# Mixer turn split in two portions per step, its first transposes in TensorE's given order

## The chip, the cores and the metric

The kernel runs on one core of one Trainium2 chip. The metric is the device time of one execution in microseconds (us). Engines are named as in the profile: PE is TensorE (matrix multiplications and transposes), PEld its weight loads, DVE is VectorE, ACT is ScalarE, POOL is GpSimd, SP issues DMA transfers.

## The reference, cut to what matters

Eight batches, eight heads of 64, 576 positions. Attention keeps, for each query, the scores that are at least its 32nd largest; what comes out (x, 576 by 512 for a batch) goes through a phase mixer.

```
scores = q @ k.T / 8;  kth = 32nd largest of each row
attn = exp(scores - max) where scores >= kth, else 0;  attn /= sum + 1e-9
x = (attn @ v), heads side by side                    # 576 x 512 per batch
theta = x @ w_theta
zr, zi = x * cos(theta), x * sin(theta)
y = w_tok_r @ zr + w_tok_i @ zi                       # over the 576 positions
u = x + y
out = u + max(u @ w_ch, 0)
```

## The kernel before

**Attention.** The work runs in units. A unit is one block `j` of 128 queries of a pair of heads `p` (five blocks, the last with 64 queries), so a batch has 20 units. `pipeline()` makes one step per unit; in step `i` the unit `i+3` gets its scores (`scores`, L259, copied out of PSUM by ACT in L268) and is folded on VectorE (`fold`, L295 to L298), unit `i+1` has its candidates picked (L303), unit `i` has its threshold found (`threshold`, L319 and L325), unit `i-1` is masked and exponentiated (L349, L351, L361), and unit `i-2` is turned: `turn` transposes the weights of each head on TensorE (`pt`, L376, four transposes, and the copy `at` out of PSUM by ACT, L378; `pq`, L386, for the rest) and calls `between()` after each of its two parts. `mix_values` multiplies by the values (`px`, L406).

**The mixer.** When a batch's 20 units are through, `mixer(...)`, a generator, is put into the list `running`. `between()` calls `advance(RATE / 2)`, so the mixer of the batch before advances twice in a step. Each call adds 4.25 to a budget, and the generator is resumed as long as the budget is above zero; each `yield` gives back the price of what has just been issued. A call to `between()` with what is issued in it is called a portion here.

The mixer has two stages. The first, called the turn here (the loop over `k`), runs over five blocks of 128 positions (the last has 64):
- the turn there: `px_s`, L595, four transposes that bring a block of x from channels to positions, into a PSUM buffer; then `normalize`, L494, on VectorE, which divides by the sums and frees that buffer;
- the turn back: `turn_back`, four transposes `px_t`, L509, and the copy `xt` by ACT, L510, which frees that buffer;
- the angles: `angles`, `pth`, L532 (L536 for the last block), four matmuls in float32 on the block that was turned back; `fraction` (L548 on ACT, L549 on VectorE) takes out whole turns.

When all five blocks are through, `trig` takes sines and cosines (L556 to L564). The second stage is the two products, 72 matmuls `py` (L647) and 32 matmuls `po` (L674) of one unit of price each, every one counted twice in the trace.

In each `k` the order before is: turn there of block `k`, turn back of block `k-1`, fraction of `k-3`, angles of `k-2`, and one `yield` of 2 or 9. Counted out with the budget, the portions of a mixer before are: 1: there 0, 1, 2, back 0, 1, angles 0; 4: there 3, back 2, angles 1; 6: there 4, back 3, angles 2; 8: back 4, angles 3; 10: angles 4; 12: the last fraction, trig, and the first four `py`. The other portions issue nothing of the mixer.

**What sets the order.** The framework's planner sorts each engine's instructions at compile time, by priority (the program's order; a mixer's instructions stand 100 places earlier, `M_REST`) and by its own times of when an instruction could start. Each engine then runs its list in that order. Instructions that got the same mark keep the program's order among themselves: `fixed` marks on TensorE the `pt` transposes, and through `fill` the angles, `py` and `po` of all mixers but the last. The transposes `px_s` and `px_t` carry no mark: the planner places them. ACT's exponentials and sines have a mark of their own (`tabled`).

**Buffers.** `pt`, `pq`, `px_s` and `px_t` share one PSUM pool, `ps_t`, of two buffers. `px`, `pth`, `py` and `po` share `ps_m`, two buffers. The scores have `ps_s`, two buffers.

**The last batch's mixer** has nothing beside it. It works with split operands (`split`), three matmuls for each one of the others, its turn back makes the parts `x_hi` (ACT, L513) and `x_lo` (VectorE, L516), and none of its instructions is marked.

Of the kernel before, what the change touches and what calls it, by code (L numbers as in the profile page):

```python
# [18 lines left out]
P = 128  # L19
# [3 lines left out]
AHEAD = 3  # L23
S_LATE = 0
RATE = 8.5
ORDER = "PTUFKSTVMXZ"
FOLDS = 4
BESTS = 4
# [16 lines left out]
def topk_attention_phase_mixer(  # L45
# [11 lines left out]
    nc = tc.nc  # L57
# [5 lines left out]
    NJ = S // P  # L63
# [22 lines left out]
    ident = const.tile([P, P], F32, name="ident")  # L86
# [86 lines left out]
    def later(n):  # L173
        return tc.high_priority(offset=-n)
# [253 lines left out]
    def two_blocks(tag, n, width, name, bufs=2):  # L428
        blocks = []
        while len(blocks) < n:  # L430
            t = wk2.tile([P, 2, S], F32R, tag=tag, name=name, bufs=bufs)
            blocks += [t[:, 0, :width], t[:, 1, :width]]
        return blocks[:n]
# [5 lines left out]
    def halve_weights(key):  # L439
        n, width = len(wts[key]), wts[key][0].shape[-1]  # L440
        hi = two_blocks("e", n, width, "w_hi", EBUFS)
        lo = []
        for c in range(n):
            if key == "th" and c == 0:
                lo.append(wk2.tile([P, S], F32R, tag="pen", name="w_lo", bufs=1)[:, :width])
            else:
                lo.append(weight_tile(F32R, width))
            halve(hi[c], lo[c], wts[key][c], nc.scalar.copy, nc.vector.tensor_sub if key == "ch" else nc.gpsimd.tensor_sub)
        w_parts[key] = hi, lo
# [3 lines left out]
    def mixer(bt, split=False, beside=False):  # L453
        bq, xt, sums, sums_rem = bt["bq"], bt["xt"], bt["sums"], bt["sums_rem"]
# [16 lines left out]
        fill = fixed if beside else lambda ins: None  # L471
# [16 lines left out]
        def normalize(k, px):  # L488
            rows, parts = (P, 1) if k < NJ else (REM, folds)
            for a in range(parts):  # L490
                cols = slice(a * DM // parts, (a + 1) * DM // parts)
                out = xs[k][a * D : a * D + rows, : DM // parts]
                hs = slice(cols.start // D, cols.stop // D)
                nc.vector.tensor_tensor(  # L494
                    out.rearrange("p (h d) -> p h d", d=D),
                    px[:rows, cols].rearrange("p (h d) -> p h d", d=D),
                    rinv[:rows, k, hs].unsqueeze(2).to_broadcast([rows, hs.stop - hs.start, D]),
                    op=ALU.mult,
                )

        def turn_back(j):
            rows, parts = (P, 1) if j < NJ else (REM, folds)
            m = NB // parts
            for a in range(parts):
                sl = slice(a * D, a * D + rows)
                pt = ps_t.tile([P, NB, P], F32, tag="t", name="px_t")
                with later(M_PE):
                    for p in range(m):
                        nc.tensor.transpose(pt[:, p, :rows], xs[j][sl, p * P : p * P + P], ident[sl, sl])  # L509
                nc.scalar.copy(xt[:, a * m : a * m + m, j * P : j * P + rows], pt[:, :m, :rows])  # L510
                if split:
                    cs = slice(j * P, j * P + rows)
                    nc.scalar.copy(x_hi[:, a * m : a * m + m, cs], pt[:, :m, :rows])  # L513
                    for p in range(a * m, a * m + m, 2):
                        pp = slice(p, p + 2)
                        nc.vector.tensor_sub(x_lo[p // 2][:, :, cs], xt[:, pp, cs], x_hi[:, pp, cs].bitcast(F32))  # L516

        def angles(j):
            th[j] = ps_m.tile([P, 512], F32, tag="m", name="pth")
            cs = slice(j * P, j * P + P) if j < NJ else slice(NJ * P, S)  # L520
            mm = []
            for p in range(NB):
                if split:
                    x = u_hi[p][:, cs], u_lo[p][:, cs]
                    mm += passes(*x, *(w[p] for w in w_parts["th"]))
                else:
                    mm.append((xt[:, p, cs], wts["th"][p]))
            with later(M_PE):
                for i, (l, r) in enumerate(mm):
                    pos = dict(start=(i == 0), stop=(i == len(mm) - 1), skip_group_check=True)  # L530
                    if j < NJ or split:
                        fill(nc.tensor.matmul(th[j][: l.shape[-1]], l, r, **pos))  # L532
                    else:
                        for a in range(2):
                            fill(
                                nc.tensor.matmul(  # L536
                                    th[j][a * D : a * D + D, :HD], l, r[:, a * HD : a * HD + HD], **pos
                                )
                            )

        def fraction(j):
            whole = wk2.tile([P, S], F32, tag="ot", name="whole", bufs=1)[:, :DM]
            if j == NJ:
                last[0] = whole
            _, zr, _ = spots(j)
            n = zr.shape[-1]
            m = zr.shape[0]
            nc.scalar.activation(whole[:m, :n], th[j][:m, :n], AF.Identity, bias=magic[:m])  # L548
            nc.vector.scalar_tensor_tensor(  # L549
                zr, whole[:m, :n], MAGIC, th[j][:m, :n], op0=ALU.subtract, op1=ALU.subtract  # L550
            )

        def trig(js):
            for j in js:
                x, zr, zi = spots(j)
                tabled(nc.scalar.activation(zi, zr, AF.Sin, scale=-TWO_PI))  # L556
                nc.scalar.activation(zr, zr, AF.Abs)
                tabled(nc.scalar.activation(zr, zr, AF.Sin, scale=-TWO_PI, bias=half_pi[: zr.shape[0]]))
                nc.gpsimd.tensor_mul(zr, x, zr)
                if split and j == NJ:  # L560
                    nc.vector.tensor_mul(z[REM : 2 * REM, 2 * NJ], x, zi)
                    halve_z(2 * NJ)
                    continue
                nc.gpsimd.tensor_mul(x if j < NJ else zi, x, zi)  # L564
                if split:
                    halve_z(NJ + j)
                    halve_z(j)
                if j == NJ:
                    for i in range(2):
                        for a in range(2):  # L570
                            nc.sync.dma_start(
                                z[i * D : i * D + D, 2 * NJ, a * HD : a * HD + HD], spots(j)[1 + i][a * D : a * D + D]
                            )
# [6 lines left out]
        if split:  # L580
            halve_weights("tok")
            halve_weights("ch")
            for i, n in enumerate(QN):
                t = wk2.tile([P, 2, NJ, n], F32R, tag=f"at{i}", name="z_hi", bufs=1)
                flat = t.rearrange("p a b n -> p (a b n)").rearrange("p (k d) -> p k d", d=DM)
                z_hi.extend(flat[:, k] for k in range(flat.shape[1]))
            z_lo += two_blocks("kh", NJ, DM, "z_lo") + two_blocks("q2", NJ, DM, "z_lo")
            z_lo.append(wk2.tile([P, S], F32R, tag="lo1", name="z_lo")[:, :DM])
        for k in range(NJ + 4):
            if k <= NJ:  # L590
                rows = P if k < NJ else REM
                px = ps_t.tile([P, DM], F32, tag="t", name="px_s")
                with later(M_PE):
                    for p in range(NB):
                        nc.tensor.transpose(px[:rows, p * P : p * P + P], xt[:, p, k * P : k * P + rows], ident)  # L595
                normalize(k, px)
            if 0 <= k - 1 <= NJ:
                turn_back(k - 1)
            if 0 <= k - 3 <= NJ:
                fraction(k - 3)  # L600
            if 0 <= k - 2 <= NJ:
                angles(k - 2)
            yield (2 if k <= NJ + 1 else 0) + (7 if 0 <= k - 2 <= NJ else 0)
        trig(range(NJ + 1))
        yield 0

# [83 lines left out]
    def pipeline():  # L690
# [46 lines left out]
        for i in range(total + 3):  # L737
# [4 lines left out]
            def keep():  # L742
                u = unit(i - 3)
                if u:
                    keep_values(u)
                    if u.j == NJ and u.p == NPAIR - 1:
                        done = B - 1 - u.bq
                        running.append(mixer(u.batch, done == 0, done > 0))

            def ahead():  # L750
# [9 lines left out]
                "Z": lambda: list(parts),  # L760
                "U": lambda: last and turn(last, unit(i - 3), lambda: advance(RATE / 2)),
                "K": keep,
# [4 lines left out]
            }  # L767
            for c in ORDER:
                steps[c]()
# [90 lines left out]
```

## Time and profile before

| what | us |
|---|---|
| median of 3 runs (1256.29 to 1263.52) | 1259.68 |
| the profiled execution, its own time | 1256.43 |
| its span, first to last instruction | 1254.7 |
| TensorE matmul busy | 1138.1 |
| VectorE busy | 1117.9 |
| ScalarE busy | 1016.3 |
| GpSimd busy | 686.5 |

Busy times are those of the whole span; the first 180 us also hold the preparation of weights and the first batch, the last 70 us the mixer of the last batch. Seven mixers run beside the attention of the next batch. A wait is idle time of an engine ahead of an instruction, with the one that released it.

### The profile page before, as it was taken

To read this page: it belongs to the slowest core of one execution; us is meant where nothing else is said; L and a number is where in the kernel's file an instruction comes from. 1 tells how busy PE (TensorE), PEld (TensorE's weight loads), DVE (VectorE), ACT (ScalarE), POOL (GpSimd) and SP (SyncE) were. 2 spreads that over 40 slices of the span, in tenths; PEclk is the share of its full clock that TensorE was granted. 3 is DMA by queue.
4 is the path that set the end of the run, shared out by engine and by line. 5 is a ranking of instruction groups with operands and counts; after the bars stand their busy time and mean duration, and the time that the engine had idled before them with its cause. 6 is when DMAs were issued, how large, how long until landed. Compare 5 with 4: busy or idle time off the path is not lost.

```text
span 1254.7 us, 22863 instructions
## 1 busy us (share of the span) xinstructions
PE 1138.1 (91%) x6293; PEld 847.9 (68%) x6293; DVE 1117.9 (89%) x5018; ACT 1016.3 (81%) x2098; POOL 686.5 (55%) x958
## 2 busy tenths in 40 slices
PE   4676678999899997999989999999989998899998
PEld 3454455777557775677757776677757775577688
DVE  7999999999998999889998989988999989995363
ACT  5799998897689977898779968898789977898361
POOL 2678875665456634566445644656455644557340
PEclk9767789999899999999999999999999999999999
DMA  6544542333323233333323333332323333210101
GB/s 165 128 131 135 152 109 53 94 86 101 89 67 76 62 109 96 78 83 86 91 52 94 86 104 87 85 90 59 102 72 95 86 94 97 68 27 11 39 1 41
DMA packets 71017, 106.12 MB, mean 85 GB/s; under 512 B 13920, under 2 KB 32608, under 8 KB 70880
## 3 DMA queue, kind: packets, MB, share of 16 engines
q1 hardware_dynamic: 70880, 104.57, 31.6%
q8 instruction: 52, 0.85, 0.3%
q14 instruction: 85, 0.70, 0.2%
HBM read 38.40 MB, written 9.44 MB: 38 GB/s over the span
## 4 chain that ended last, share of the span: by engine, by line
PE 41%; DVE 28%; ACT 18%; DMA 4%; POOL 4%; issue 3%; SPq 1%; ACTq 0%; DVEq 0%; POOLq 0%
PE py L647 13%; PE pth L532 7%; DVE best L319 6%; DVE lst L325 6%; PE px L406 5%; PE ps_score L259 5%; DVE lst L303 5%; ACT e L361 5%; PE pt L376 4%; ACT pen L349 3%; DVE lo L296 3%; ACT e L268 3%; PE po L674 2%; POOL e L351 2%; DVE ps_score L295 2%
## 5 line engine op out<-in xcount | busy, mean ns | idle before, releaser
L351 POOL TENSOR_TENSOR e<-e,pen 128x576 f32<-128x576 f32 x288 | 365.8, 1285 | 129.8 <-ACT pen L349 127.2
L319 DVE MAX8 best<-lst 128x8 f32<-128x102 f32 (+3 forms) x1152 | 287.2, 291 | 9.7 <-POOL lim L330 9.2
L647 PE MATMUL py<-w,z 128*128 128x288 f32 x1008 | 265.5, 407 | 0.6 <-ACT xt L418 0.6
L361 ACT ACTIVATE e<-e,lim 128x576 f32<-128x576 f32 x288 | 225.0, 783 | 26.4 <-POOL e L351 24.4
L349 ACT ACTIVATE pen<-e,lim 128x576 bf16<-128x576 f32 x288 | 210.5, 775 | 31.8 <-POOL lim L330 31.4
L325 DVE MATCH_REPLACE8 lst<-best,lst 128x102 f32<-128x102 f32 (+2 forms) x864 | 232.4, 277 | 0.1
L259 PE MATMUL ps_score<-kh,q 128*128 128x288 f32 x512 | 185.5, 377 | 31.8 <-ACT e L268 14.6
L303 DVE MAX8 lst<-lo 128x8 f32<-128x72 f32 (+1 forms) x864 | 210.1, 295 | 0.0
L647 PEld LDWEIGHTS py<-w,z 128*128 128x128 f32 x1008 | 182.2, 190 | 41.2 <-ACT xt L418 1.3
L376 PE MATMUL pt<-ident,e 128*128 128x128 f32 x1152 | 181.1, 283 | 27.0 <-ACT e L361 14.8
L376 PEld LDWEIGHTS pt<-ident,e 128*128 128x128 f32 x1152 | 140.5, 145 | 66.3 <-ACT e L361 18.1
L268 ACT COPY e<-ps_score 128x576 f32<-128x576 f32 x256 | 160.7, 640 | 29.6 <-PE ps_score L259 24.0
L378 ACT COPY at<-pt 128x512 f32<-128x512 f32 x256 | 148.2, 589 | 36.1 <-PE pt L376 35.5
L406 PE MATMUL px<-at,vt 128*64 128x320 f32 (+1 forms) x1024 | 164.0, 437 | 5.6 <-ACT at L381 3.1
L259 PE MATMUL ps_score<-kl,q 128*128 128x288 f32 x512 | 152.5, 312 | 0.4 <-DMA kl<-raw 0.4
L259 PEld LDWEIGHTS ps_score<-kh,q 128*128 128x128 f32 x512 | 101.6, 198 | 61.8 <-ACT e L268 22.3
L406 PEld LDWEIGHTS px<-at,vt 128*64 128x64 f32 x1024 | 79.4, 145 | 68.7 <-issue 15.1
L674 PE MATMUL po<-xt,w 128*128 128x288 f32 x448 | 124.0, 408 | 1.0 <-DVE ot L628 0.8
L296 DVE TENSOR_TENSOR lo<-ps_score,e 128x576 f32<-128x576 f32 (+1 forms) x160 | 110.2, 689 | 0.0
L532 PE MATMUL pth<-w,xt 128*128 128x512 f32 x224 | 109.7, 623 | 0.0
L259 PEld LDWEIGHTS ps_score<-kl,q 128*128 128x128 f32 x512 | 102.7, 201 | 8.6 <-issue 3.7
L295 DVE TENSOR_TENSOR ps_score<-ps_score,e 128x288 f32<-128x288 f32 (+1 forms) x160 | 68.3, 427 | 37.8 <-ACT e L268 35.3
(130 smaller groups left out, 1914.4 us busy)
## 6 DMA issues: line engine op xcount, KB each, us to landing
kh<-hi SPq DMA_DIRECT2D x124, 144.0 KB, 2.8
kl<-raw SPq DMA_DIRECT2D x124, 144.0 KB, 2.7
raw<-in_qT_dram SPq DMA_DIRECT2D x31, 288.0 KB, 2.9
raw<-in_kT_dram SPq DMA_DIRECT2D x31, 288.0 KB, 3.2
q<-hi SPq DMA_DIRECT2D x62, 144.0 KB, 2.7
q<-raw SPq DMA_DIRECT2D x62, 144.0 KB, 2.7
vt<-in_v_dram SPq DMA_DIRECT2D x32, 256.0 KB, 3.6
out_dram<-ot SPq DMA_DIRECT2D x28, 288.0 KB, 2.1
```

What stands on the lines that cost most here:

```text
L259: nc.tensor.matmul(out[:, at : at + n], l, r, start=(i == 0), stop=(i == len(mm) - 1), skip_group_check=True)
L268: nc.scalar.copy(u.x[:, :, keys], u.ps[:, :, :HS])
L303: nc.vector.max(u.lst[:, w, QS + i * 8 : QS + i * 8 + 8], u.lo1[:, w, lo:hi])
L319: nc.vector.max(top[:, w, best], part[w])
L325: nc.vector.match_replace(out=rest, in_to_replace=top[:, w, best], in_values=part[w], imm_value=LOWEST)
L349: nc.scalar.activation(pen[:, w], u.x[:, w], AF.Relu, bias=u.lim[:, w, 0:1], scale=-STEEP)
L351: nc.gpsimd.tensor_sub(u.x[:, w], u.x[:, w], pen[:, w])
L361: nc.scalar.activation(u.x[:, w], u.x[:, w], AF.Exp, bias=u.lim[:, w, 1:2], scale=SCALE, accum_out=acc)
L376: fixed(nc.tensor.transpose(pt[:, c], e[:, w, at0 : at0 + P], ident))
L406: nc.tensor.matmul(px[sl, :n], pr["vt"][:, kb, sl], pr["at"][:, a, kb], start=(kb == 0), stop=False, skip_group_check=True)
L532: fill(nc.tensor.matmul(th[j][: l.shape[-1]], l, r, **pos))
L647: fill(nc.tensor.matmul(py[:, :HS], l, r, start=(i == 0), stop=(i == len(mm) - 1)))
```

## The change

The turn's loop is issued in two portions per step. The first has the turn there of block `k`, the fraction of block `k-3` and the angles of block `k-2`; the second has the turn back of block `k-1`. Each gives back `TURN`, 4.25, all that a call adds. The transposes of the turn there get the mark `fixed`, through `fill`, in all mixers but the last.

Counted out in the same way, the portions become: 1: there 0; 2: there 1, back 0; 3: there 2, angles 0; 4: back 1; 5: there 3, angles 1; 6: back 2; 7: there 4, angles 2; 8: back 3; 9: angles 3; 10: back 4; 11: angles 4; 12: the last fraction, trig, and the first five `py`. In the last mixer only the order in which the loop issues its work is another.

```diff
@@ -23,6 +23,7 @@
 AHEAD = 3
 S_LATE = 0
 RATE = 8.5
+TURN = 4.25
 ORDER = "PTUFKSTVMXZ"
@@ -586,21 +587,23 @@
         for k in range(NJ + 4):
             if k <= NJ:
                 rows = P if k < NJ else REM
                 px = ps_t.tile([P, DM], F32, tag="t", name="px_s")
                 with later(M_PE):
                     for p in range(NB):
-                        nc.tensor.transpose(px[:rows, p * P : p * P + P], xt[:, p, k * P : k * P + rows], ident)
+                        fill(nc.tensor.transpose(px[:rows, p * P : p * P + P], xt[:, p, k * P : k * P + rows], ident))
                 normalize(k, px)
-            if 0 <= k - 1 <= NJ:
-                turn_back(k - 1)
             if 0 <= k - 3 <= NJ:
                 fraction(k - 3)
             if 0 <= k - 2 <= NJ:
                 angles(k - 2)
-            yield (2 if k <= NJ + 1 else 0) + (7 if 0 <= k - 2 <= NJ else 0)
+                yield TURN
+            if 0 <= k - 1 <= NJ:
+                turn_back(k - 1)
+            yield TURN if k <= NJ + 1 else 0
         trig(range(NJ + 1))
         yield 0
```

## Rows read from the trace of the kernel before

**Rows 1.** The page's first part: busy us, share of the span, instructions.
```profile
span 1254.7 us, 22863 instructions
...
PE 1138.1 (91%) x6293; PEld 847.9 (68%) x6293; DVE 1117.9 (89%) x5018; ACT 1016.3 (81%) x2098; POOL 686.5 (55%) x958
```

**Rows 2.** Windows: the turns of the mixers beside attention; busy us, PEclk granted share.
```profile
178.40:231.90 53.50, 45.58 (x232) 29.21 (x232) 51.90 (x230) 47.96 (x95) 34.65 (x45) 0.94 0.29 75
331.70:380.50 48.80, 43.63 (x227) 27.31 (x226) 46.12 (x208) 38.52 (x77) 27.26 (x38) 0.93 0.33 79
478.90:525.80 46.90, 41.58 (x222) 26.26 (x221) 42.73 (x189) 35.12 (x70) 23.61 (x31) 0.96 0.32 79
625.70:672.50 46.80, 42.22 (x228) 27.77 (x228) 44.90 (x204) 36.72 (x73) 25.22 (x35) 0.96 0.35 87
769.70:814.60 44.90, 42.01 (x226) 26.95 (x225) 44.66 (x202) 36.13 (x73) 24.55 (x33) 0.96 0.36 89
910.90:955.90 45.00, 41.15 (x231) 26.73 (x230) 44.37 (x195) 38.76 (x77) 26.76 (x35) 1.00 0.35 88
...
sum 332.50, PE 297.33 PEld 190.92 DVE 320.35 ACT 269.72 POOL 186.71; mean PE 42.48 PEld 27.27 DVE 45.76 ACT 38.53 POOL 26.67
```

**Rows 3.** Windows between those turns (231.9 to 1054.6, six stretches), summed.
```profile
sum 590.30, PE 577.40 PEld 452.46 DVE 548.87 ACT 501.47 POOL 319.60; mean PE 96.23 PEld 75.41 DVE 91.48 ACT 83.58 POOL 53.27
```

**Rows 4.** TensorE's waits, whole span: us in total, times, longest us.
```profile
PE px_s L595 <- DVE z L494: 6.7, 6, 3.1
PE px_s L595 <- ACT at L378: 4.6, 7, 2.0
...
PE pt L376 <- ACT xt L510: 3.8, 6, 1.3
PE px_t L509 <- DVE z L494: 3.4, 3, 1.7
PE pt L376 <- DVE z L494: 3.4, 3, 2.8
PE px_t L509 <- ACT xt L510: 3.2, 2, 2.3
...
PE pq L386 <- DVE end L494: 2.5, 2, 2.3
...
PE px_s L595 <- ACT xt L510: 2.0, 2, 1.3
PE pq L386 <- ACT xt L510: 2.0, 2, 1.3
```

**Rows 5.** Timeline of TensorE in the second mixer's turn: start, us.
```profile
335.87 0.66 PE L509 MATMUL px_t<-ident,z 128*128 128x128 f32 x4 [1.45 <-DVE z L494]
337.49 0.84 PE L595 MATMUL px_s<-ident,xt 128*128 128x128 f32 x4 [0.97 <-DVE z L494]
339.28 0.47 PE L509 MATMUL px_t<-ident,z 128*128 128x128 f32 x1 [0.94 <-ACT xt L510]
339.54 1.91 PE L532 MATMUL pth<-w,xt 128*128 128x512 f32 x2
...
352.20 3.60 PE L532 MATMUL pth<-w,xt 128*128 128x512 f32 x8
```

**Rows 6.** VectorE's waits, whole span: us in total, times, longest us.
```profile
DVE ps_score L295 <- ACT e L268: 35.3, 30, 3.7
...
DVE z L494 <- PE px_s L595: 5.9, 6, 2.4
```

**Rows 7.** Windows: the last mixer's turn; columns as in rows 2.
```profile
1187.00:1204.70 17.70, 16.93 (x91) 13.20 (x91) 10.67 (x20) 12.95 (x23) 2.60 (x2) 1.00 0.01 1
```

**Rows 8.** Timeline of the last mixer's turn, around one turn back.
```profile
1194.79 0.58 ACT L510 COPY xt<-px_t 128x512 f32<-128x512 f32 x1
...
1195.25 0.60 ACT L513 CAST x_hi<-px_t 128x512 fp32r<-128x512 f32 x1
...
1196.15 0.74 DVE L516 TENSOR_TENSOR x_lo<-xt,x_hi 128x256 fp32r<-128x256 f32 x2
```

## Prediction

> **What bounds the kernel now.** I began with the page: TensorE and VectorE are busy 91% and 89% of the span [rows 1], so neither is plainly the bound, and the stages have to be taken apart. I cut the span into windows: the seven turns that run beside attention, and what lies between them. Between the turns TensorE is busy 577.40 of 590.30 us and VectorE 548.87 [rows 3]: there TensorE sets the pace, with 13 us idle in six stretches, and VectorE waits for scores (the copy L268 behind TensorE's products, 35.3 us over the span) [rows 6]. In the turns it is the other way round on paper: TensorE is busy 297.33 of 332.50 us, so it is idle for 35.2 us, and VectorE is busy 320.35, idle for 12.15 [rows 2]. A turn stage is thus one in which both are nearly full, VectorE a little more.
>
> What TensorE waits for in the turns is read from its waits. The nine rows in which the turn's own work is late, or makes others late, add up to 31.6 us [rows 4]; the last mixer can hold no more than 0.77 of it, all its idle time [rows 7], so these waits are nearly all of the 35.2 us idle in the seven turns. They fall into three kinds:
> - The chain without distance, 21.2 us: the turn there waits for a buffer that `normalize` frees (6.7) or that a turn back's copy frees (2.0), the turn back for `normalize` (3.4) or for a copy (3.2), and `pt` and `pq` stand behind a late `normalize` (3.4 and 2.5).
> - `pt` and `pq` waiting for the copy L510 to free a buffer, 3.8 and 2.0, 5.8 together.
> - The turn there waiting for the copy of `pt`, 4.6 in 7 waits.
>
> The timeline shows why the first kind arises: portion 1 issues three turns there, two turns back and the first angles at once, and each stands behind the one before: 1.45, 0.97 and 0.94 us idle within 4 us [rows 5].
>
> A second loss hangs on it. In the same place two angle matmuls take 1.91 us, while eight take 3.60 us some 12 us later, 0.95 against 0.45 each [rows 5]: TensorE runs at the lower of its two levels, 1.2 instead of 2.4 GHz. The granted clock is 0.94, 0.93, 0.96, 0.96 and 0.96 in the first five turns, 1.00 in the sixth [rows 2]. Missing share times length gives 3.2, 3.4, 1.9, 1.9 and 1.8, 12.2 us of full-speed work lost. In the second turn it fell right after the gaps of portion 1.
>
> **The change part by part.** No instruction is added or removed on any engine. Trig, with its work on GpSimd and its DMA issues on SP, stays in portion 12, so neither queue is passed; ten turns (five there, five back) and their angles are issued in other portions.
>
> 1. *The chain gets distance.* Angles 0 came in the portion of their own turn back; now each block's angles stand one portion behind its turn back, and its turn back one to three portions behind its turn there. A turn lasts 47.5 us on average for 12 portions [rows 2], so a portion is about 4 us of cover, against waits of 0.9 to 3.1 us [rows 4, 5]. Blocks 1 to 4 had more portions between turn back and angles before than after (two or three, now one), so not all of this is won. Of the 21.2 I take two thirds, -14. The ends are 0 (the cover isn't there) and -21.2.
> 2. *`pt` and `pq` behind the turn back's copy.* The turn back still sits next to `pt` or `pq` and uses the same two buffers. I leave it: 0. Ends -5.8 and +5.8 (as often again, since a turn back now has a portion to itself in front of `pq`).
> 3. *The turn there in given order.* It can no longer be placed early; it comes right behind a `pt` and needs the other of the two buffers, which the copy of an earlier `pt` must have freed. Behind it stand, in TensorE's order, the angles and the next `pt`, and behind that ACT's copy and `px`. Seven waits took 4.6 us, 0.66 each [rows 4]; there are 35 such turns. I take twice as many as now: +4.6. Ends: none left, -4.6, and all 35 at 0.66, 23 in all, +18.4.
> 4. *The clock.* If gaps of portion 1 go, the lower level should go with most of them. The sixth turn has 3.85 us idle at 1.00 [rows 2], so gaps need not bring it down. I take half, -6; ends 0 and -12.2. The Trainium skill (TensorE: Matmul & The Clock Gate, Part 1) says that a monitor sets the array's rate by how busy it has been lately; that fits these rows, and by it all 12.2 us would come back once the array stays busy, which would make the forecast some 6 us lower. The sum does without it.
> 5. *The end of the turn.* Angles 4 move from portion 10 to 11, while trig and the first `py` stay in 12. Between angles 4 and the next unit's `pt`, one `pt` less and one `py` more are issued. I take 0; it lies within the uncertainty of item 3.
> 6. *The last mixer.* Angles now go ahead of the turn back of the next block, so for every second block TensorE may stand through that block's copy, `x_hi` and `x_lo`: from 1194.79 to 1196.89, 2.1 us [rows 8]. Two blocks can meet it, +4.2; the planner can place an idle transpose there, and TensorE is idle for 0.77 us in that turn now [rows 7], the most that could be won. I take +1.5; ends -0.8 and +4.2.
>
> TensorE in the turns: -14 + 0 + 4.6 - 6 = -15.4 us. Not all of it reaches the end: VectorE has only 12.15 us free in these windows [rows 2], and I cut the gain there: -12. With the last mixer -10.5. Against the profiled execution's own time, 1256.43 (its span and 1.7 us around it), that is 1245.9. This execution lies 3.25 below the median of the runs, 1259.68; on the median the forecast is 1249.
>
> **The rivals.**
>
> *VectorE is the bound in the turn, and nothing comes through.* It is busy 96% of these windows, and in the fifth 44.66 of 44.90 us [rows 2]; TensorE's time won there would be spent waiting for a folded unit to free the scores' buffers. Against it: between the turns VectorE has 41.4 us free [rows 3], and a TensorE that leaves the turn earlier starts the products earlier. Then only the turns in which VectorE has room give anything: the second and third, 2.7 and 4.2 us idle. The time would be 1253 to 1260, say 1257. The Trainium skill (Trainium Kernel Development and Optimization, Performance Expectations) says that a matmul's busy time is a poor measure and the weight loads' busy share a good one. By that TensorE is loaded to 57% in the turns (190.92 of 332.50) and to 77% between them, and it wouldn't be the bound in the turn. Chance 0.17.
>
> *The split doesn't happen on the engine.* `px_t` carries no mark, and the planner may put it right behind `px_s` again. The waits then change places. Two or three us less, 1257 as well. Chance 0.09.
>
> *The given order costs more than the distance gives: slower.* The place is the turn there behind `pt`. Gains of items 1 and 4 are 20 us; divided by 35 that is 0.57 us. From an average added wait of 0.57 us at each turn there it decides, and the waits seen are 0.66 on average and 2.0 at the longest [rows 4]. `normalize` stands in VectorE's order, and where the transposes come late VectorE waits too (5.9 us in 6 waits now) [rows 6], in a stage in which it has nothing to spare. At 0.9 us each, 31.5 - 20 and the last mixer's 1.5 give +13, 1273; at 0.7, 1266. For it speaks that a marked instruction can't be moved around a late one; against it that the angles behind the turn there give `normalize` 3.6 us of cover [rows 5] before the next `pt` asks for a buffer. Chance 0.20.
>
> **How the numbers follow.** The forecast has 0.54. A measurement of this kernel can tell some 0.5% from no change, 6.3 us: faster is below 1253.4, slower above 1266.0. The first two rivals mostly fall in between, the third mostly above. So faster 0.54, same 0.26, slower 0.20. The forecast's own range is 1238 (all of items 1 and 4 less item 3's 4.6 is 28.8; 12.15 of it in the windows, half of the rest by VectorE's room between the turns, and 0.8 in the last mixer: 21.3) to 1255 (half of item 1, no clock: -10.6 + 4.6 + 1.5). For 8 in 10 I leave out the best tenth below 1239 and the worst above 1268, which takes in the first two rivals and the near part of the third.
>
> **What would show it.** Right: the rows of `px_s`, `px_t`, `pt` and `pq` waiting for L494 and L510 fall from 27 to about 13 us; the granted clock in the first five turns is 0.98 or more; windows of a turn get 1 to 3 us shorter, and VectorE's waits for L268 between the turns don't grow. Item 3 is wrong if `px_s` waits for L378 more than 10 us. The first rival is right if TensorE's waits for the fold (L298) grow in the turns by what the others lose. Item 6 is wrong if the last 68 us of the span move by more than 4. The prediction as a whole is wrong if TensorE's idle time in the turns stays above 30 us, or if it falls and the span doesn't.

## The result and the profile after

The changed kernel takes 1245.73 us (median of 4 runs, 1245.3 to 1247.91) against 1258.32 us for the kernel before in the same runs: a ratio of 0.9895, 95% interval 0.9872 to 0.9917. The forecast was 1249, the range 1239 to 1268. The forecast gain was 10.5 us, the measured one 12.6 between the medians. The profiled execution of the changed kernel took 1245.62 us; the forecast on that scale was 1245.9. All medians are of fast runs: one run of the turn spread over 15 portions, further down, took 1923.37 us at a granted clock of 0.653 and is left out.

The page's first part for the changed kernel (its lines stand one to three lower than before: L597 is the turn there, L510 the turn back, L511 its copy, L495 `normalize`, L379 the copy of `pt`, L650 `py`):

```profile
span 1243.8 us, 22867 instructions
...
PE 1134.8 (91%) x6293; PEld 844.3 (68%) x6293; DVE 1114.8 (90%) x5018; ACT 1016.8 (82%) x2098; POOL 686.1 (55%) x958
```

The work is the same on every engine [rows 1]; the span is 10.9 us shorter. Where it went is seen in the windows. First the turns of the seven mixers beside attention, columns as in [rows 2]:

```profile
175.80:225.40 49.60, 43.82 (x228) 27.88 (x228) 48.62 (x216) 42.48 (x86) 26.52 (x38) 0.97 0.33 83
330.00:376.90 46.90, 43.07 (x238) 27.96 (x237) 46.86 (x217) 41.01 (x84) 25.93 (x38) 1.00 0.37 93
...
761.20:803.30 42.10, 40.51 (x227) 26.55 (x227) 41.87 (x185) 36.16 (x72) 22.46 (x30) 1.00 0.36 91
...
sum 314.70, PE 292.52 PEld 189.22 DVE 309.05 ACT 266.97 POOL 166.14; mean PE 41.79 PEld 27.03 DVE 44.15 ACT 38.14 POOL 23.73
```

The seven turns are 17.8 us shorter. TensorE is idle for 22.2 us in them instead of 35.2, VectorE for 5.7 instead of 12.15, and the granted clock is 1.00 in all but the first. Work lost to the clock, missing share times length, fell from 12.2 to 1.5 us (0.03 of 49.6). Then the stretches between the turns, three of those before and the same three after, with the sum of all six:

```profile
231.90:331.70 99.80, 97.25 (x560) 76.51 (x559) 97.52 (x460) 82.44 (x177) 53.01 (x81) 1.00 0.36 95
...
525.80:625.70 99.90, 96.73 (x551) 75.30 (x550) 93.61 (x431) 84.12 (x178) 53.29 (x80) 1.00 0.31 81
...
955.90:1054.60 98.70, 96.21 (x547) 74.78 (x546) 90.70 (x431) 83.52 (x178) 53.49 (x81) 1.00 0.32 85
```

```profile
225.40:330.00 104.60, 99.16 (x551) 77.21 (x550) 94.60 (x436) 83.76 (x176) 56.93 (x81) 0.97 0.32 84
...
518.70:619.80 101.10, 97.69 (x551) 75.41 (x550) 93.64 (x434) 85.00 (x179) 56.23 (x83) 0.98 0.31 83
...
945.70:1046.40 100.70, 97.88 (x550) 76.97 (x549) 92.15 (x432) 84.36 (x178) 56.42 (x84) 0.98 0.31 83
sum 598.20, PE 581.30 PEld 453.38 DVE 555.16 ACT 504.10 POOL 336.37; mean PE 96.88 PEld 75.56 DVE 92.53 ACT 84.02 POOL 56.06
```

Here 7.9 us are given back: TensorE is idle for 16.9 us instead of 12.9 [rows 3], and the lower clock, which before did not occur between the turns, now costs 0.03 of 104.6, 0.02 of 101.1 and 0.02 of 100.7, 7.2 us. These three stretches are 4.8, 1.2 and 2.0 us longer than before, which is all of the 7.9. The first turn begins 2.6 us earlier, and behind the last of these turns 1.6 us are lost: -17.8 + 7.9 - 2.6 + 1.6 is the -10.9 of the span. The 2.6 us lie ahead of the first mixer and are not shown to come from the change: in the thirteen kernels that change the turn, this one included, the first `px_s` starts anywhere from 177.34 to 181.42 us, against 179.89 before.

TensorE's waits over the whole span, to set beside [rows 4]:

```profile
PE pq L387 <- ACT at L379: 17.7, 14, 2.4
PE pt L377 <- ACT e L362: 17.5, 13, 2.5
...
PE pt L377 <- ACT at L379: 8.9, 11, 1.4
...
PE px_t L510 <- ACT at L379: 3.8, 3, 2.6
PE py L650 <- POOL z L565: 2.4, 2, 1.8
...
PE px_s L597 <- DVE z L495: 1.1, 2, 0.8
...
PE pth L533 <- ACT xt L511: 0.7, 1, 0.7
PE pt L377 <- ACT xt L511: 0.6, 1, 0.6
...
PE pq L387 <- ACT xt L511: 0.5, 1, 0.5
PE px_s L597 <- ACT at L379: 0.5, 1, 0.5
```

The waits of the turn for itself are nearly gone: of the 21.2 us of chain waits 1.1 is left, with 0.7 new at the angles. What has grown is the wait for the copy of `pt` (L379), at `pq`, `pt` and now at the turn back. The timeline of TensorE in the second mixer's turn shows how both come about, beside [rows 5]:

```profile
331.48 0.60 PE L597 MATMUL px_s<-ident,xt 128*128 128x128 f32 x4
...
333.75 0.66 PE L377 MATMUL pt<-ident,e 128*128 128x128 f32 x4 [1.02 <-ACT at L379]
...
335.54 0.66 PE L510 MATMUL px_t<-ident,z 128*128 128x128 f32 x4
...
340.57 0.66 PE L597 MATMUL px_s<-ident,xt 128*128 128x128 f32 x4 [0.44 <-ACT rem L388]
341.06 3.60 PE L533 MATMUL pth<-w,xt 128*128 128x512 f32 x8
```

Turn there 0 to turn back 0 takes 4 us instead of 2.6 (333.23 to 335.87 before), filled with attention; the angles of block 0 run as one piece of eight in 3.60 us, at full clock, where two took 1.91 before. Between the two, `pt` now waits 1.02 us for a buffer. The last mixer's turn, beside [rows 7]:

```profile
1175.60:1193.80 18.20, 17.06 (x92) 13.45 (x92) 10.87 (x20) 13.09 (x23) 2.59 (x2) 1.00 0.00 1
```

### The profile page after: what moved, and what is told of

It reads as the page before. It is cut to its first block, busy times and chain, and to the rows that moved or that the text cites. A ratio compares the mean times of both kernels' runs of the same rounds, so it can differ in the third digit from the quotient of the medians.

```text
span 1243.8 us, 22867 instructions
## 1 busy us (share of the span) xinstructions
PE 1134.8 (91%) x6293; PEld 844.3 (68%) x6293; DVE 1114.8 (90%) x5018; ACT 1016.8 (82%) x2098; POOL 686.1 (55%) x958
## 4 chain that ended last, share of the span: by engine, by line
PE 43%; DVE 24%; ACT 22%; DMA 4%; issue 3%; POOL 2%; SPq 1%; ACTq 0%; POOLq 0%; DVEq 0%
PE py L650 16%; PE px L407 5%; PE pth L533 5%; PE ps_score L260 5%; DVE lst L326 5%; DVE best L320 5%; PE pt L377 5%; DVE lst L304 4%; ACT e L362 4%; ACT pen L350 4%; ACT e L269 3%; DVE lo L297 2%; PE po L677 2%; ACT at L379 2%; DVE ps_score L296 1%
## 5 line engine op out<-in xcount | busy, mean ns | idle before, releaser
L320 DVE MAX8 best<-lst 128x8 f32<-128x122 f32 (+3 forms) x1152 | 284.9, 289 | 12.1 <-POOL lim L331 11.6
L650 PE MATMUL py<-w,z 128*128 128x288 f32 x1008 | 268.0, 409 | 3.3 <-POOL z L565 2.4
L362 ACT ACTIVATE e<-e,lim 128x576 f32<-128x576 f32 x288 | 225.0, 782 | 22.6 <-POOL e L352 21.9
L260 PE MATMUL ps_score<-kh,q 128*128 128x288 f32 x512 | 182.2, 371 | 35.7 <-ACT e L269 16.1
L650 PEld LDWEIGHTS py<-w,z 128*128 128x128 f32 x1008 | 183.0, 191 | 44.7 <-POOL z L565 2.8
L379 ACT COPY at<-pt 128x512 f32<-128x512 f32 x256 | 149.5, 589 | 27.3 <-PE pt L377 26.3
L260 PE MATMUL ps_score<-kl,q 128*128 128x288 f32 x512 | 149.9, 308 | 0.3 <-DMA kl<-raw 0.3
L533 PE MATMUL pth<-w,xt 128*128 128x512 f32 x224 | 100.9, 593 | 0.7 <-ACT xt L511 0.7
L213 POOL TENSOR_TENSOR raw<-raw,hi 128x1152 fp32r<-128x1152 f32 x31 | 82.1, 2647 | 29.8 <-ACT hi L212 29.8
```

What stands on the lines that cost most here:

```text
L260: nc.tensor.matmul(out[:, at : at + n], l, r, start=(i == 0), stop=(i == len(mm) - 1), skip_group_check=True)
L320: nc.vector.max(top[:, w, best], part[w])
L362: nc.scalar.activation(u.x[:, w], u.x[:, w], AF.Exp, bias=u.lim[:, w, 1:2], scale=SCALE, accum_out=acc)
L379: nc.scalar.copy(at[:, w, :, q0 : q0 + P], pt)
L650: fill(nc.tensor.matmul(py[:, :HS], l, r, start=(i == 0), stop=(i == len(mm) - 1)))
```

## Experiments

Twelve kernels were run. Each ratio is to the kernel before, in runs on the same chip; the changed kernel ran only with the first set, so a difference from its 1245.73 us sets medians of different sets side by side, in which the kernel before took 1258.00 to 1260.85 us. By the ratios the four differences used below (11.7, 24.5, 24.3 and 42 us) would be 11.6, 24.8, 23.4 and 43.8. Windows are cut by the same rule for all: a turn from 1.5 us ahead of the first `px_s` to the first `py`.

### The two parts of the change apart

The mark alone, on the kernel before:

```diff
-                        nc.tensor.transpose(px[:rows, ...], ..., ident)
+                        fill(nc.tensor.transpose(px[:rows, ...], ..., ident))
```

> The kernel before with the mark on the turn there alone. My theory (distance between the steps of the turn gives the gain, the mark costs a little): no gain, 1258 to 1270 us, portion 1 still shows its chain of waits (L595, L509 and the angles) and the lower clock after it. Rival (the fixed place of the turn there gives the gain): 1244 to 1250 us, with the waits of px_s and px_t for L494 and L510 gone although portion 1 is as before.

Measured: 1253.53 us, ratio 0.9963 (0.9949 to 0.9977). My theory said no gain, and failed. The rival's mechanism is there only in part. The sum of its turns and two of its waits

```profile
sum 333.20, PE 296.86 PEld 191.62 DVE 320.57 ACT 272.16 POOL 189.30; mean PE 42.41 PEld 27.37 DVE 45.80 ACT 38.88 POOL 27.04
```

```profile
PE px_s L595 <- ACT at L378: 11.4, 13, 1.9
...
PE px_s L595 <- DVE z L494: 7.3, 5, 3.2
```

show TensorE as idle in the turns as before (36.3 us) and `px_s` still waiting for `normalize`, while `px_t`, `pt` and `pq` no longer do (9.3 us before [rows 4], 0.3 here). The wait of `px_s` for the copy of `pt` has grown from 4.6 to 11.4 (0.88 us each, 13 times); I had forecast 9.2 for the mark. The profiled span is 2.4 us shorter than that before, but the turns are 0.7 longer: the stretches between them are 3.4 shorter (586.9 instead of 590.3), nearly all of it in TensorE's busy time, at a granted clock of 1.00 in both, with 15 matmuls fewer in them and 12 more in the turns. So this one profile doesn't show where the 4.5 us of the medians come from.

The two portions alone, on the changed kernel:

```diff
-                        fill(nc.tensor.transpose(px[:rows, ...], ..., ident))
+                        nc.tensor.transpose(px[:rows, ...], ..., ident)
```

> The changed kernel without the mark: the two portions alone. My theory: all of the gain and the mark's price back, 1241 to 1248 us, TensorE idle in the seven turns 18 to 24 us. Rival (the mark is needed, since the planner otherwise pulls the turn there forward): 1252 to 1260 us, with waits of px_s for L494 or L378 back.

Measured: 1252.11 us, 0.9954 (0.9936 to 0.9972). Less than half the gain: my "all of it" failed, and the rival's number just caught it. Its turns:

```profile
sum 333.30, PE 297.79 PEld 192.91 DVE 322.20 ACT 270.67 POOL 169.99; mean PE 42.54 PEld 27.56 DVE 46.03 ACT 38.67 POOL 24.28
```

```profile
PE pq L387 <- ACT at L379: 15.4, 13, 2.4
...
PE pt L377 <- ACT at L379: 11.3, 13, 1.9
...
PE px_t L510 <- ACT at L379: 4.2, 6, 1.1
PE pt L377 <- DVE z L495: 3.9, 3, 2.1
PE px_s L597 <- ACT xt L511: 3.1, 4, 1.0
PE pth L533 <- ACT xt L511: 2.9, 1, 2.9
```

35.5 us idle, as before. The order between the steps is new, and the chain's rows fall from 21.2 to 9.2 us (3.9 and 3.1 above, and 1.6 and 0.6 of `px_t` and `px_s` for `normalize`). But the angles now wait 2.9 us for their block, and the waits for the copy of `pt`, which before came to 4.6 us in the turns, all at `px_s`, are 15.9 us there, at `pt`, `px_t`, `pq` and `px_s`. What this kernel gains over the kernel before is by its rows mostly the clock: its turns show 0.97, 1.00, 0.96, 0.97, 1.00, 1.00 and 1.00, 4.8 us lost instead of 12.2, and none between them. So the shorter idle time of the turn, 22.2 us, came only with both parts; the gains of the parts, 4.5 and 5.9 us, come to about four fifths of the 12.6 together.

### The crowded first portion

The kernel before, with the prices of its `yield` changed so that blocks 0 and 1 take a portion each, and the order kept:

```diff
-            yield (2 if k <= NJ + 1 else 0) + (7 if 0 <= k - 2 <= NJ else 0)
+            yield (4.25, 4.25, 8.5, 8.5, 8.5, 8.5, 4.25, 0)[k]
```

> The kernel before, its order within a block kept and no mark, but blocks 0 and 1 take a portion each, so that portion 1 no longer holds three turns there, two back and the first angles. My theory that most of the loss sits in the crowded portion 1 and in the clock that falls after it: two thirds of the gain, 1248 to 1252 us, and the granted clock in the first five turns 0.98 or more. Rival (the turn back in a portion of its own matters, in every block): 1255 to 1260 us.

Measured: 1258.65 us, 0.9997 (0.9981 to 1.0013): no change, my expectation failed. The turns did get shorter, as the chain of portion 1 went:

```profile
sum 325.80, PE 297.62 PEld 191.72 DVE 308.62 ACT 263.09 POOL 163.46; mean PE 42.52 PEld 27.39 DVE 44.09 ACT 37.58 POOL 23.35
```

28.2 us idle. But four of the seven still ran at 0.93 to 0.96, and three stretches between them gave back the rest, the second the most (0.97 of 102.5 us):

```profile
374.90:477.40 102.50, 99.27 (x550) 77.77 (x549) 96.42 (x457) 87.49 (x184) 59.13 (x90) 0.97 0.34 90
...
sum 597.90, PE 583.12 PEld 456.07 DVE 557.16 ACT 508.85 POOL 341.00; mean PE 97.19 PEld 76.01 DVE 92.86 ACT 84.81 POOL 56.83
```

The waits of portion 1 that I had blamed for the clock were gone, and the clock fell all the same, after others: in the turns behind the turn back's copy above all (`pt` 8.4 us in 9 waits), and in the three stretches between them each time after `px` had waited 2.0 to 2.3 us for a copy of `pt` (L381) just ahead of the next turn. That row has grown from 3.1 us:

```profile
PE px L406 <- ACT at L381: 8.2, 6, 2.3
```

The edit does one thing more than it was meant for: counted out, every later block comes one portion later too, and angles 4 move from portion 10 to 11, as in the change. What that alone costs here wasn't run.

### The last mixer

The changed kernel, whose last mixer alone keeps the order of before:

```diff
+            if split and 0 <= k - 1 <= NJ:
+                turn_back(k - 1)
             if 0 <= k - 3 <= NJ:
                 fraction(k - 3)
...
-            if 0 <= k - 1 <= NJ:
+            if not split and 0 <= k - 1 <= NJ:
                 turn_back(k - 1)
```

> The changed kernel, but the last mixer keeps the order of before. The last mixer's turn took 17.7 us before and 18.2 us after. My term for it was +1.5 us: then 1244 to 1245 us. Rival (the planner makes up for the order): within 0.6 us of the changed kernel, its last turn 17.7 us, and nothing else moves.

Measured: 1247.42 us, 0.9914 (0.9889 to 0.9939), not to be told from the changed kernel. Its last turn:

```profile
1177.70:1195.40 17.70, 16.93 (x91) 13.04 (x90) 10.40 (x20) 12.68 (x23) 2.60 (x2) 1.00 0.00 1
```

17.7 us, as [rows 7]; the order costs 0.5 us there, not 1.5. The rival was right on the turn; on the time it wasn't borne out, as this median is 1.7 us above the changed kernel's and not within 0.6, a difference that the intervals don't tell from none.

### Which engine sets the pace in the turn

Three kernels add work to the changed one. Each turn there transposed twice into the same buffer:

```diff
-                    for p in range(NB):
+                    for p in (*range(NB), *(range(NB) if beside else ())):
```

> The changed kernel with the transposes of each turn there done twice into the same buffer, in the seven mixers beside attention: some 0.44 us more of TensorE for each of 35 turns there, 15 us. TensorE as the bound, in the turns too: 13 to 18 us more than the changed kernel, 1259 to 1264 us. The first rival of the prediction (VectorE is the bound in the turns and TensorE has room there): 0 to 5 us more, 1246 to 1251 us.

Measured: 1257.46 us, 0.9987 (0.9972 to 1.0002): 11.7 us more than the changed kernel for some 15 us of work, under my range but far above the rival's.

Each `normalize` twice, 28 more of 0.68 us and 14 more of 0.41, 24.8 us:

```diff
                 normalize(k, px)
+                if beside:
+                    normalize(k, px)
```

> The changed kernel with each normalize done twice, in the seven mixers beside attention: 3.5 us more of VectorE for each mixer, 25 us in all, and each turn there's buffer held 0.7 us longer. VectorE as the bound in the turns: 18 to 25 us more, 1264 to 1271 us. TensorE as the bound, VectorE's room between the turns taking it up: 2 to 9 us more, 1248 to 1255 us.

Measured: 1270.27 us, 1.0092 (1.0058 to 1.0127): 24.5 us more, nearly every microsecond of it, as forecast if VectorE is the bound in the turns. To see whether it was VectorE's time or the longer way from turn there to turn back, VectorE's half of the fraction was done twice for the four full blocks, 28 more of 0.68 us, 19 us:

```diff
-            nc.vector.scalar_tensor_tensor(zr, ...)
+            for _ in range(2 if beside and j < NJ else 1):
+                nc.vector.scalar_tensor_tensor(zr, ...)
```

> The changed kernel with the VectorE half of the fraction (L550 of the changed kernel) done twice for the four full blocks, in the seven mixers beside attention: 2.7 us more of VectorE for each mixer, 19 us in all, in the turns, but not between a turn there and its turn back. If doubling normalize cost 24.5 us because VectorE is full in the turns: 14 to 19 us more than the changed kernel, 1260 to 1265 us. If it cost that because it lengthened the chain from turn there to turn back: 2 to 7 us more, 1248 to 1253 us.

Measured: 1270.06 us, 1.0081 (1.0053 to 1.011): 24.3 us more for 19 us of work that isn't on that way, above even the range for a full VectorE. Its turns and the stretches between:

```profile
sum 342.60, PE 308.55 PEld 200.52 DVE 331.85 ACT 267.55 POOL 167.15; mean PE 44.08 PEld 28.65 DVE 47.41 ACT 38.22 POOL 23.88
...
sum 591.30, PE 575.24 PEld 449.08 DVE 555.38 ACT 507.20 POOL 337.36; mean PE 95.87 PEld 74.85 DVE 92.56 ACT 84.53 POOL 56.23
```

VectorE is busy 331.85 of 342.60 us in the turns, and the 36 us that it has free between them took up nothing. So in the turn VectorE is full and time added to it reaches the end; of TensorE's some three quarters did. It is a stage with two bounds.

The difference between three quarters and more than all may be the clock's. Missing share times length, in the turns and between them, is 8.7 us in the changed kernel, 5.6 with the turn there twice, 10.0 with `normalize` twice and 13.4 with the fraction twice. Less those differences the three would cost 14.8 for 15, 23.2 for 24.8 and 19.6 for 19. That is an estimate from shares of two digits and one profile each.

### Three attempts to do better

The last turn back in portion 8, so that angles 4 come two portions ahead of trig and `py`, as before:

```diff
                 angles(k - 2)
-                yield TURN
-            if 0 <= k - 1 <= NJ:
+                yield TURN if k <= NJ + 1 else 2 * TURN
+            if 0 <= k - 1 < NJ:
                 turn_back(k - 1)
-            yield TURN if k <= NJ + 1 else 0
+            if k == NJ:
+                turn_back(NJ)
+            yield TURN if k <= NJ else 0
```

> The changed kernel with the last turn back in portion 8 beside the one before it, and so the last angles in portion 10, as before, two portions ahead of trig and the products; nothing else moves. If part of the gain is given back because trig and the first product follow the last angles too closely (TensorE's waits for L565, 2.4 us, and for L362 between the turns, 4.6 us): 1241 to 1244 us, and both waits fall to under 2 us together. Rival (they move elsewhere, or the crowded portion 8 costs as much): 1245 to 1249 us.

Measured: 1244.55 us, 0.9882 (0.9847 to 0.9917). The lowest of all, but its interval covers the changed kernel's. The product's wait for L565 fell from 2.4 to 1.3 us and that of `pt` for L362 between the turns from 4.6 to 3.0: in the direction expected, but not to under 2 us together, and too little to settle it.

```profile
PE py L652 <- POOL z L565: 1.3, 1, 1.3
```

The mark on the turn back too:

```diff
-                        nc.tensor.transpose(pt[:, p, :rows], ...)
+                        fill(nc.tensor.transpose(pt[:, p, :rows], ...))
```

> The changed kernel with the mark on the turn back too. If a given order is worth something by itself because the planner's placing of single transposes between waiting ones is what costs (the mark alone gave 0.9963): 1240 to 1244 us. My first theory, in which a mark costs freedom: 1247 to 1253 us, with px_t waiting for L494.

Measured: 1246.1 us, 0.9896 (0.9862 to 0.9931): neither theory; no gain and no cost of the mark can be told there.

The turn spread over 15 portions, with denser products so that the mixer ends in time:

```diff
-RATE = 8.5
-TURN = 4.25
+RATE = 9.5
+TURN = 4.75
...
-            yield TURN if k <= NJ + 1 else 0
+            yield (2 if 1 <= k <= NJ else 1) * TURN if k <= NJ + 1 else 0
```

> The changed kernel with an empty portion after the turns back of blocks 0 to 3, so that the turn takes 15 portions instead of 11, and with 4.75 instead of 4.25 products in a portion, so that the mixer ends where it ended. If VectorE, full in the turns and with 43 us free between them, is what the turns cost: 1238 to 1243 us. Rival (TensorE is the bound in both stages, so moving VectorE's load gains nothing and denser products crowd the attention's transposes): 1246 to 1252 us.

Measured: 1296.08 us, 1.0287 (1.0244 to 1.0331). The opposite of my expectation, and beyond the rival's. The same prices on the kernel with the last turn back moved up (the edit of the first attempt above), every turn back in two portions:

```diff
-            yield TURN if k <= NJ else 0
+            yield (2 if k >= 1 else 1) * TURN if k <= NJ else 0
```

> The same spreading on the kernel whose last turn back stands in the portion of the one before it. If both add up: 1235 to 1242 us. Rival: no better than without the spreading, 1244 to 1250 us.

Measured: 1292.91 us, 1.0263 (1.0229 to 1.0298). To tell the longer turn from the denser products, the changed kernel got the prices alone, with no empty portions:

```diff
-RATE = 8.5
-TURN = 4.25
+RATE = 9.5
+TURN = 4.75
```

> The changed kernel with 4.75 instead of 4.25 products in a portion and the turn as it is in the change: one half of the spread turn, which took 1296.5 us. If the denser products are what cost it: 1280 to 1297 us. If the longer turn (15 portions) is what cost it: 1243 to 1252 us.

Measured: 1288.01 us, 1.0243 (1.0211 to 1.0274). The prices alone, and with them the density of the products, cost 42 us, most of the loss. Its stretches between the turns, and two of VectorE's waits:

```profile
sum 610.30, PE 586.63 PEld 453.92 DVE 522.42 ACT 476.88 POOL 318.48; mean PE 97.77 PEld 75.65 DVE 87.07 ACT 79.48 POOL 53.08
```

```profile
DVE ps_score L296 <- ACT e L269: 62.5, 32, 6.2
DVE xt L626 <- PE py L650: 40.5, 23, 6.3
```

VectorE is idle for 88 us between the turns instead of 43, waiting for scores (62.5 us over the span; the changed kernel has 20.8) and for the products themselves (40.5; 27.0), while in the turns it is busy 335.53 of 338.50 us. Between the turns it does 32.7 us less work than in the changed kernel, in the turns 26.5 more, and the turns are 23.8 us longer. So what it loses beside the dense products is made up in turns that are already full. Sparser products, the other direction, were not tried.

## Why the prediction came out, step by step

The time was right to 0.3%, and the change works where the prediction put it, in the turn. The terms were right only in sum, and that the profiled execution came within 0.3 us of the forecast is in part luck: 2.6 us of its 10.9 lie ahead of the first turn, where no term stood. The turns and what lies between them gave 9.9 of the 12 us forecast there. Of the signs named beforehand, the rows waiting for L494 and L510 fell from 27 to 2.2 us instead of 13, and the granted clock was 0.97, 1.00, 1.00, 1.00 and 1.00 in the first five turns.

1. *The chain gets distance*: -14 forecast; from 21.2 to 1.8 us in the changed kernel's rows, with 0.4 of `px_s` behind another copy some -19, near the best end. But the portions alone, which give the same distance, left 9.2 of the 21.2, and the turns' idle time at 35.5 us. Distance in the program is worth what the planner leaves of it.
2. *`pt` and `pq` behind the turn back's copy*: 0 forecast, 5.8 to 1.1 us.
3. *The mark's price*: this is the step that failed. I forecast more waits of `px_s` for the copy of `pt`, +4.6. In the mark alone they came (4.6 to 11.4 us), and yet the kernel got faster; in the whole change they fell to 0.5, and the wait for that copy sits at `pq`, `pt` and `px_t`. All four together went from 19.0 (4.6 at `px_s` [rows 4], none at `px_t`, and two rows of the same view) to 30.9 us:

```profile
PE pq L386 <- ACT at L378: 9.8, 7, 2.4
...
PE pt L376 <- ACT at L378: 4.6, 6, 1.5
```

So the two buffers are the price, some 12 us instead of 4.6, paid by others than I named. Nor is it the mark's alone: the portions without the mark have 32.5 us of these waits (15.4, 11.3, 4.2 and 1.6), and in the turns by themselves they are 4.6 us before, 11.4 with the mark, 15.9 with the portions and 15.7 with both. I had put this at nothing for the portions. Beside them the mark is a gain, some 6 us (1252.11 to 1245.73): with it the chain's rows fall from 9.2 to 1.1 us and the angles' wait for their block from 2.9 to 0.7.
4. *The clock*: -6 forecast; -10.7 in the turns and +7.2 between, -3.5 in the profiled execution. What failed here is that it hangs on portion 1: with that portion emptied, the clock fell in other places. In the first stretch between the turns of the changed kernel it fell behind two waits of the first products, and the rows there show what it costs, 2.91 us for six `py` against 2.11 for eight a little later (granted clock 0.59 over 236.0 to 242.8 us, 1.00 behind it):

```profile
233.78 0.75 PE L650 MATMUL py<-w,z 128*128 128x288 f32 x2 [1.83 <-POOL z L565]
236.08 1.11 PE L377 MATMUL pt<-ident,e 128*128 128x128 f32 x4 [1.55 <-ACT e L362]
...
238.91 2.91 PE L650 MATMUL py<-w,z 128*128 128x288 f32 x6
...
242.09 2.11 PE L650 MATMUL py<-w,z 128*128 128x288 f32 x8
```

In the third and the sixth stretch it fell elsewhere, just ahead of the next turn, behind waits of the scores for the fold and for their copy (0.69 over 614.9 to 618.3 us, 0.70 over 1041.6 to 1045.0):

```profile
612.84 0.40 PE L260 MATMUL ps_score<-kh,q 128*128 128x288 f32 x1 [2.78 <-DVE lo L299]
...
1038.54 0.41 PE L260 MATMUL ps_score<-kh,q 128*128 128x288 f32 x1 [1.57 <-ACT e L269]
```

Each of these drops to 1.2 GHz came after TensorE had stood still, though not every wait brought one: the sixth turn before had 3.85 us idle at 1.00. By the Trainium skill (TensorE: Matmul & The Clock Gate, Part 1) a monitor sets the array's rate by how busy it has been lately; the trace agrees so far. That all 12.2 us would come back was not borne out, as the gaps moved.
5. *The end of the turn*: 0 forecast. Trig and the first product follow the last angles by one portion now. The two waits shown at the first products, 1.83 and 1.55 us, with the drop behind them, are what can be put to it; they stand in the first of the six stretches, which alone gives back 4.8 of the 7.9 us. The waits for L565 and L362 between the turns are 7.0 us in all. TensorE's idle time between the turns rose by 4.0 us.
6. *The last mixer*: +1.5 forecast, +0.5 measured, and gone where its own experiment takes the order back.

Of the rivals, the first had its premise right: VectorE is the bound in the turn, as two experiments show. I cut the gain for that, from 15.4 to 12; the turns and the stretches between gave 9.9, and in TensorE's account that is -13.0 and +4.0 of idle time and -0.9 of busy time, so that little of the -3.5 of clock is seen there. Its conclusion was wrong: it allowed a gain only in the second and the third turn, and six of the seven got shorter, the fifth, where VectorE had 0.24 us free, by 2.8. In VectorE's account the 17.8 us are 6.5 of idle time, halved, and 11.3 of its work, 320.35 to 309.05, while the stretches between hold 6.3 more; why that work stands elsewhere now isn't shown. By the Trainium skill (Trainium Kernel Development and Optimization, Performance Expectations) the weight loads' busy share is a good measure of TensorE where the matmuls' is a poor one, and at 60% of the turns now it would leave TensorE room there. The trace agrees that TensorE isn't the only bound, but 11.7 of 15 us added to it reached the end, so the room isn't free. The second rival describes in part what the portions alone did: the chain was halved, but other waits kept the idle time where it was. The third rival's waits, of `px_s` for the copy of `pt`, came to 11.4 us where the mark stood alone on the kernel before, and even there they did not decide.

What stays open: why the mark alone gives 4.5 us at the same idle time, how the planner's placing of unmarked transposes turns distance back into waits, and how much of the 12.6 us is the clock's. One profile of each kernel is not enough for it: eleven runs of one kernel differ by 3 us, the twenty-four of the kernel before beside them by 8.

## What to carry to other kernels

Where a planner places work between given pieces, a new order in the program is a wish; check on the engine that it was kept, and give the step that the others wait for a fixed place. A stage in which two engines are nearly full charges for time lost on either: measure it by doubling a piece of the work of each, because the busy shares alone don't say how much reaches the end. And count what a saved wait turns into: here 17.8 us were won in the turns and 7.9 given back behind them.

## What the runs showed of the hardware

- In the changed kernel the granted clock was 0.59 over 236.0 to 242.8 us, behind waits of 1.83 and 1.55 us, and six `py` took 2.91 us there against 2.11 for eight a little later. It was 0.69 and 0.70 over two short stretches behind waits of 2.78 and 1.57 us. Taking away one group of waits moved the drops elsewhere.
- VectorE's time added in the turn cost 1.0 us for one (24.5 for 24.8) and in another place of the turn 1.3 (24.3 for 19); TensorE's 0.8 (11.7 for 15). The granted clock differed between these kernels, by enough, on the estimate above, to explain the spread.
- Prices of 4.75 for 4.25 and 9.5 for 8.5 in the interleaving cost 42 us, at the same work and the same number of instructions on every engine.
